# A Nystrom-attention and two-MLP kernel: heads grouped by parity, landmark products as eight 64x32 tiles, first q and k transposed a head at a time

## The chip, the cores and the metric

The kernel runs on one core of a Trainium2 chip. The metric is the device time of one execution in microseconds (us). Before the change the median of 3 runs is 896.05 us (895.35 to 901.98). About 1% (9 us) is what a measurement of this kernel can tell from no change.

## The reference

Nystrom attention with 32 landmarks per head feeds two MLPs; 4 batches, 8 heads of 64, 576 positions, all fp32.

```python
def _attn_ref(q, k, v):                      # (4, 8, 576, 64)
    q_lm = q.reshape(B, H, 32, 18, D).mean(axis=3)
    k_lm = k.reshape(B, H, 32, 18, D).mean(axis=3)
    A, Bm, C = sm(q, k_lm), sm(q_lm, k_lm), sm(q_lm, k)   # scaled softmax
    Z = Bm.T / (norm1(Bm) * norm_inf(Bm) + 1e-06)
    for _ in range(6):
        Z = 2 * Z - Z @ Bm @ Z
    return A @ Z @ C @ v
x = attn_out                                  # (2304, 512)
h = x @ w_in;   x = (h * sigmoid(h)) @ w_out              # 512 -> 2048 -> 512
h = x @ w2_in;  out = (h * tanh(softplus(h))) @ w2_out
```

## The kernel before, in words

**Stages.** A batch (b = 0 to 3) is two units (g = 0, 1) of four heads, and a unit is two pairs p of two heads. Per unit: q and k are loaded and transposed so that the head dimension lies on the partitions (tiles qT, kT); landmark sums (lm, qb); the product c of landmark queries with all keys; its softmax; a transposition of it (cp, ct); norms and the product with v (nb, cv); six Newton steps (nw, rv; attn_newton, L411); a last product wk, from which wt is made; and beside it the product a of all queries with landmark keys, transposed and normalised into ath (and its low part atl).

**Landmark products.** A is never multiplied with the 512 columns of the attention's output. u_steps (L518) multiplies wt, one row block of Z C v per head, into the first MLP's input weights: for every pair jp of 128-column blocks of w_in (8 pairs, 4 batches, so 32 blocks of work), a tile u of 128 x 512 in one PSUM bank. A tile wt holds two heads on 128 partitions, block-diagonal: wk is computed for both partition halves (L441), and the mask own2 (L446) keeps each head's own half, so half of what L531 multiplies is zero. Each u_steps call makes eight fp32 matmuls with 128 rows, 64 columns of weights and 128 moving columns; an fp32 matmul is two passes in the trace, so 16 rows of L531 a call. The result is copied by ACT (L541 for b = 0; for the others L546 as the rounded high part uw, and DVE's subtraction L548 as the low part).

**First MLP.** For b = 0, ha (L628) multiplies uf with ath, and ya (L829) multiplies the activated blocks gs with w_out, in two turns over 16 blocks; y_out writes the sums. For b = 1 to 3 the values are split in high and low parts (fp32r), and each block step t of the main loop has six passes h (L608), the activation on ACT, DVE and POOL, and twelve passes y (L608). Weights come as float64 words and are converted by POOL, ACT and DVE (L590 to L599) in three raw buffers; wsplit_stream (L790) splits w_out for b = 1 on (wh, wl). convert2 converts the second MLP's weights to DRAM in the background. The second MLP (hh, o) follows from about 480 us on and is not touched, but for a tile's name.

**What sets the order.** All of b = 0, b = 1 and the conversions is written as streams of steps with planned costs and dependencies, and interleave (L45) picks at each turn the step with the lowest score: when it could begin, plus WASTE times the idle time it would make, plus the stream's delay (the last number of each entry at L843 to L866). The program's order on every engine is what it picked; each engine then runs its own list in order. In the main loop u_all (L551) calls u_steps for the next batch in every second step, and attention steps of the batch after that run between (banks 5 and 7).

**Transpositions of b = 0.** attn_transposes (L219) makes, per half tile (96 x 3 rows of two heads), six fp32 matmuls against the identity, the two heads into partitions 0 to 63 and 64 to 127 of one bank (L242), and one ACT copy of 128 x 288 (L248). There are 16 half tiles, 8 a unit. From b = 1 on, both heads go in one PE transposition (L246). The q half tiles of a unit use one bank and the k half tiles another.

## Time and profile before

| | |
|---|---|
| median of 3 runs | 896.05 us |
| the profiled execution | 899.86 us, of which the span from its first to its last instruction is 898.1 us |
| busy share: PE, DVE, ACT, POOL | 96%, 73%, 53%, 33% |
| mean granted TensorE clock | 0.982 of full speed |

The profiled execution is 3.8 us above the median. An instruction row has its start, its duration, its engine, line and tiles. [...]

### The profile page before, as it was taken

How to read it: one execution, taken by the hardware profiler on the slowest of the kernel's cores; microseconds unless marked ns; L12 is line 12 of the kernel's file. 1: busy time of each engine (PE TensorE's matmuls, PEld its weight loads, DVE VectorE, ACT ScalarE, POOL GpSimd, SP SyncE). 2: the span in 40 equal slices, each digit the busy share in tenths (PEclk: the TensorE clock that was granted, in tenths of full speed). 3: DMA queues.
4: the chain of work that ended last, by engine and by line, in shares of the span. 5: the costliest groups of instructions: out<-in, count | busy, mean ns of one | idle time of the engine just before them, and what ended most of it. 6: DMA issues, size and time to landing. Idle time of an engine off the chain costs nothing.

```text
span 898.1 us, 15048 instructions
## 1 busy us (share of the span) xinstructions
PE 863.3 (96%) x5440; PEld 762.3 (85%) x5440; DVE 651.1 (73%) x1265; ACT 472.7 (53%) x1013; POOL 293.9 (33%) x334
## 2 busy tenths in 40 slices
PE   7799989999999998899999999999999999999997
PEld 5567767779998998899899889899999999999896
DVE  3878858676576968742364997787787787797776
ACT  3656546345344646653564555554554554555544
POOL 2211333015343545532433542242242242242221
PEclk8899989999999999999999999999999999999999
DMA  8645663433454576720562210110110110000000
GB/s 230 169 97 169 189 192 101 81 81 88 100 149 101 143 224 222 244 87 17 161 181 68 79 45 1 36 35 1 36 36 1 37 36 1 35 1 1 36 1 35
DMA packets 95354, 79.62 MB, mean 89 GB/s; under 512 B 52528, under 2 KB 80688, under 8 KB 95280
## 3 DMA queue, kind: packets, MB, share of 16 engines
q1 hardware_dynamic: 95280, 78.67, 30.6%
q8 instruction: 42, 0.69, 0.3%
q14 instruction: 32, 0.26, 0.1%
HBM read 60.82 MB, written 17.83 MB: 88 GB/s over the span
## 4 chain that ended last, share of the span: by engine, by line
PE 79%; DVE 8%; DMA 5%; ACT 3%; POOL 2%; issue 2%; SPq 1%; ACTq 0%; DVEq 0%; POOLq 0%
PE hh L608 21%; PE o L1098 20%; PE y L608 14%; PE h L608 7%; PE ya L829 5%; PE u L531 4%; PE ha L628 3%; DMA q<-in_q_dram 2%; PE nw L423 1%; DVE z L1036 1%; DMA w2r<-w2c 1%; DMA k<-in_k_dram 1%; PE cv L374 1%; POOL rawt L590 1%; PE c L307 1%
## 5 line engine op out<-in xcount | busy, mean ns | idle before, releaser
L1042 POOL TENSOR_TENSOR g<-z,g 128x384 fp32r<-128x384 f32 x94 | 96.0, 1022 | 256.0 <-ACT g L1039 253.6
L608 PE MATMUL y<-g,wh 128*128 128x288 f32 x768 | 162.4, 302 | 6.8 <-ACT g L659 2.9
L1098 PE MATMUL o<-wh,g 128*128 128x512 f32 x576 | 165.7, 395 | 2.9 <-ACT g L1039 1.9
L660 POOL TENSOR_TENSOR g<-g,g 128x288 fp32r<-128x288 f32 x96 | 82.4, 858 | 184.9 <-ACT g L659 143.0
L608 PEld LDWEIGHTS y<-g,wh 128*128 128x128 f32 x768 | 124.5, 190 | 12.0 <-ACT g L659 3.1
L608 PE MATMUL hh<-yl,wi2h 128*128 128x384 f32 x384 | 129.6, 337 | 0.0
L608 PE MATMUL hh<-yh,wi2h 128*128 128x384 f32 x384 | 129.2, 336 | 0.0
L608 PE MATMUL hh<-yh,wi2l 128*128 128x384 f32 x384 | 129.1, 336 | 0.0
L1098 PEld LDWEIGHTS o<-wh,g 128*128 128x128 f32 x576 | 106.0, 188 | 23.3 <-ACT g L1039 4.1
L1039 ACT CAST g<-z 128x384 fp32r<-128x384 f32 x96 | 49.3, 514 | 133.6 <-DVE z L1038 133.6
L608 PE MATMUL y<-g,wl 128*128 128x288 f32 x384 | 114.6, 298 | 0.0
L1025 DVE TENSOR_SCALAR e<-hh 128x384 f32<-128x384 f32 x96 | 53.5, 557 | 64.2 <-PE hh L608 63.9
L608 PE MATMUL h<-ath,uw 128*128 128x288 f32 x384 | 95.1, 302 | 0.0
L658 DVE SCALAR_TENSOR_TENSOR g<-th,h 128x288 f32<-128x288 f32 x96 | 43.0, 447 | 55.8 <-ACT th L657 54.3
L1098 PE MATMUL o<-wl,g 128*128 128x512 f32 x288 | 81.7, 391 | 0.0
L1026 ACT ACTIVATE e<-e 128x384 f32<-128x384 f32 x96 | 50.4, 525 | 51.4 <-DVE e L1025 51.2
L608 PEld LDWEIGHTS hh<-yl,wi2h 128*128 128x128 f32 x384 | 72.1, 188 | 3.7
L608 PEld LDWEIGHTS hh<-yh,wi2h 128*128 128x128 f32 x384 | 72.1, 188 | 3.7
L608 PEld LDWEIGHTS y<-g,wl 128*128 128x128 f32 x384 | 73.0, 190 | 0.0
L1036 DVE SCALAR_TENSOR_TENSOR z<-z,r 128x384 f32<-128x384 f32 x96 | 70.0, 729 | 3.3
L608 PEld LDWEIGHTS hh<-yh,wi2l 128*128 128x128 f32 x384 | 72.1, 188 | 0.0
L608 PEld LDWEIGHTS h<-ath,uw 128*128 128x128 f32 x384 | 68.1, 191 | 3.6 <-issue 3.0
(165 smaller groups left out, 1631.7 us busy)
## 6 DMA issues: line engine op xcount, KB each, us to landing
rawi<-in_moe_w_in_dram SPq DMA_DIRECT2D x16, 512.0 KB, 5.6
rawo<-in_moe_w_out_dram SPq DMA_DIRECT2D x16, 512.0 KB, 3.6
rawt<-in_moe_w_in_dram SPq DMA_DIRECT2D x16, 512.0 KB, 4.7
w2c<-ct SPq DMA_DIRECT2D x32, 256.0 KB, 2.6
rawt<-in_moe_w_out_dram SPq DMA_DIRECT2D x16, 512.0 KB, 3.8
w2r<-w2c SPq DMA_DIRECT2D x32, 256.0 KB, 2.8
v<-in_v_dram SPq DMA_DIRECT2D x32, 144.0 KB, 3.1
ysc<-yo SPq DMA_DIRECT2D x32, 144.0 KB, 1.9
```

Source lines behind the costliest of these rows:

```text
L531: pe.matmul(ub[64 * p : 64 * p + 64, jj, g], wt[:, p].rearrange("a h m -> a (h m)"), wc[2 * jp + jj][:, (2 * g + p) * P : (2 * g + p + 1) ...
L608: pe.matmul(o, a, b_, start=first and i == 0, stop=last and i == n - 1)
L628: pe.matmul(hb[:, :HB], uw[j // 2][:, j % 2, g], ath[0][:, g, hf * HB : (hf + 1) * HB], start=g == 0, stop=g == 1)
L658: dve.scalar_tensor_tensor(g2, th, 1.0, hb[:, :HB], op0=ALU.add, op1=ALU.mult)
L660: eng.tensor_tensor(gl, g2, gh.bitcast(F32), op=ALU.subtract)
L829: pe.matmul(yb[hf, m][:, :HB], wof[j][:, m * P : (m + 1) * P], gst[j // 2][:, j % 2, hf], start=j == 0, stop=j == NF - 1,)
L1025: dve.tensor_scalar(e, h, 20.0, None, op0=ALU.min)
L1026: ins = act.activation(e, e, AF.Exp)
L1036: dve.scalar_tensor_tensor(z, z, -2.0, r, op0=ALU.add, op1=ALU.mult)
L1039: act.copy(gh, z)
L1042: eng.tensor_tensor(gl, z, gh.bitcast(F32), op=ALU.subtract)
L1098: pe.matmul(obank[i][c], a[:, c * P : (c + 1) * P], w, start=j == 0 and k == 0, stop=j == NF - 1 and k == 2,)
```

## The change

Heads are put in units by parity: unit g has the heads 2i + g, so a 128-row block of w_in holds one head of each unit, that of unit 0 on partitions 0 to 63 and that of unit 1 on 64 to 127. wk is then computed for one half only and copied without a mask, and u_steps makes eight fp32 matmuls with 64 rows, 32 columns of weights and 256 moving columns: four heads give four column strips, two units two row halves and two PSUM banks, a bank each. The two blocks of w_in of a pair lie in one tile (wcp, first_in). Each call's two banks are copied by two ACT instructions of 128 x 256 in place of one of 128 x 512, and subtracted by two of DVE. The transpositions of b = 0 become PE transpositions of one head each (64 x 96, six a half tile), into partitions 0 to 63 of two banks; ACT copies one, DVE the other, each 64 x 288. Banks of the transpositions: (0, 6), (1, 7) for unit 0's q and k, (3, 5), (4, 5) for unit 1's. The planner's WASTE and most delays are other numbers, which moves work in the first 200 us.

```diff
-WASTE = 1.33
+WASTE = 0.7
...
-        h0 = 4 * g + 2 * p
+        heads = [2 * (2 * p + h2) + g for h2 in range(2)]
...
-                yield Step([("pe", 0.55 if b == 0 else 0.3)], deps)
+                if b == 0:
+                    yield Step([("pe", 0.5), ("dve", 0.4)], deps, ("tr", b, g, nm, p, hf))
+                else:
+                    yield Step([("pe", 0.3)], deps)
...
-                pt = bank(bk, f"tr{u}{p}{ti}{hf}")
-                for r in range(3):
-                    c = 3 * hf + r
-                    cols = slice(r * PT, (r + 1) * PT)
-                    if b == 0:
+                halves = slice(hf * HB, (hf + 1) * HB)
+                if b == 0:
+
+                    pts = [bank(bk[h2], f"tr{u}{p}{ti}{hf}{h2}") for h2 in range(2)]
+                    for r in range(3):
                         for h2 in range(2):
-                            pe.matmul(
-                                pt[64 * h2 : 64 * h2 + 64, cols], src[:, h2, c, :], ident[:PT, :PT], start=True, stop=True
+                            pe.transpose(
+                                pts[h2][:D, r * PT : (r + 1) * PT], src[:, h2, 3 * hf + r, :], ident[:PT, :PT]
                             )
-                    else:
-                        pe.transpose(pt[:, cols], src[:, c].rearrange("a h d -> a (h d)"), ident[:PT, :PT])
-                yield Step([("act", 0.4)], (), ("tr", b, g, nm, p, hf))
-                act.copy(dst[:, hf * HB : (hf + 1) * HB], pt[:, :HB])
+                    act.copy(dst[:D, halves], pts[0][:D, :HB])
+                    dve.tensor_copy(dst[D:, halves], pts[1][:D, :HB])
+                else:
+                    pt = bank(bk, f"tr{u}{p}{ti}{hf}")
+                    for r in range(3):
+                        pe.transpose(
+                            pt[:, r * PT : (r + 1) * PT],
+                            src[:, 3 * hf + r].rearrange("a h d -> a (h d)"),
+                            ident[:PT, :PT],
+                        )
+                    yield Step([("act", 0.4)], (), ("tr", b, g, nm, p, hf))
+                    act.copy(dst[:, halves], pt[:, :HB])
...
-        for i in range(n):
-            for h2 in range(2):
-                pe.matmul(wk[64 * h2 : 64 * h2 + 64, i, :P], rv[:, i, w:], bt["bb", i], start=True, stop=True)
+        for i, g in enumerate(gs):
+            pe.matmul(wk[64 * g : 64 * g + 64, i, :P], rv[:, i, w:], bt["bb", i], start=True, stop=True)
         yield Step([("dve", 0.3)], (), ("wt", b, gs[-1]))
         for i, g in enumerate(gs):
             pl, tag = (wp, f"gt{g + 1}") if b == 0 else (ap, f"wt{g}")
-            wt = pl.tile([P, 2, 2, M], F32, tag=tag, name=f"wt{b}{g}")
-            dve.tensor_tensor(
-                wt,
-                wk[:, i, :P].rearrange("a (p h m) -> a p h m", p=2, h=2),
-                own2[:, None, :, None].to_broadcast([P, 2, 2, M]),
-                op=ALU.mult,
-            )
+            wt = pl.tile([P, 4, M], F32, tag=tag, name=f"wt{b}{g}")
+            sl = slice(64 * g, 64 * g + 64)
+            dve.tensor_copy(wt[sl].rearrange("a h m -> a (h m)"), wk[sl, i, :P])
             units[b, g]["wt"] = wt
...
-            deps += [("wc", 2 * jp), ("wc", 2 * jp + 1), ("ath", 0, 1)] + ([("u", 0, jp - 2)] if jp > 1 else [])
+            deps += [("wc", 2 * jp), ("wc", 2 * jp + 1), ("ath", 0, 1)] + ([("u", 0, jp - 1)] if jp else [])
         elif b == 1:
             deps += [("y", 1, 2 * jp + 1)] + ([("u", 1, jp - 2)] if jp > 1 else [])
-        yield Step([("pe", 0.9)], deps)
-        ub = atbank(f"u{b}{jp}").rearrange("a (j g f) -> a j g f", j=2, g=2)
-        for g in range(2):
-            wt = units[b, g]["wt"]
-            for jj in range(2):
-                for p in range(2):
-                    pe.matmul(
-                        ub[64 * p : 64 * p + 64, jj, g],
-                        wt[:, p].rearrange("a h m -> a (h m)"),
-                        wc[2 * jp + jj][:, (2 * g + p) * P : (2 * g + p + 1) * P],
-                        start=True,
-                        stop=True,
-                    )
+        yield Step([("pe", 0.5)], deps)
+        ub = [atbank(f"u{b}{jp}{g}") for g in range(2)]
+
+        for h in range(4):
+            for g in range(2):
+                sl = slice(64 * g, 64 * g + 64)
+                pe.matmul(
+                    ub[g][32 * h : 32 * h + 32, : 2 * P].rearrange("a (j f) -> a j f", j=2),
+                    units[b, g]["wt"][sl, h],
+                    wcp[jp][sl, :, h * P : (h + 1) * P],
+                    start=True,
+                    stop=True,
+                )
         if b == 0:
-            yield Step([("act", 0.6)], (), ("u", 0, jp))
+            yield Step([("act", 0.8)], (), ("u", 0, jp))
             uw[jp] = wp.tile([P, 2, 2, P], F32, tag=f"u{jp}", name=f"uf{jp}")
-            act.copy(uw[jp], ub)
+            for g in range(2):
+                act.copy(uw[jp][:, g].rearrange("a j f -> a (j f)"), ub[g][:, : 2 * P])
             return
-        yield Step([("act", 0.6)])
+        yield Step([("act", 0.8)])
         ut = wp.tile([P, 2, 2, 2, P], F32R, tag=f"g{jp}", name=f"uw{b}_{jp}")
         uh, ul = ut[:, 0], ut[:, 1]
-        act.copy(uh, ub)
-        yield Step([("dve", 0.7)], (), ("u", b, jp))
-        dve.tensor_tensor(ul, ub, uh.bitcast(F32), op=ALU.subtract)
+        for g in range(2):
+            act.copy(uh[:, g].rearrange("a j f -> a (j f)"), ub[g][:, : 2 * P])
+        yield Step([("dve", 0.8)], (), ("u", b, jp))
+        for g in range(2):
+            dve.tensor_tensor(
+                ul[:, g].rearrange("a j f -> a (j f)"),
+                ub[g][:, : 2 * P],
+                uh[:, g].bitcast(F32).rearrange("a j f -> a (j f)"),
+                op=ALU.subtract,
+            )
         uw[jp] = (uh, ul)
...
+    wcp = {}
+
+    def first_in(j):
+
+        if j // 2 not in wcp:
+            wcp[j // 2] = wp.tile([P, 2, 512], F32, tag=f"wc{j // 2}", name=f"wc{j // 2}")
+        return wcp[j // 2][:, j % 2]
...
-            pe.matmul(hb[:, :HB], uw[j // 2][:, j % 2, g], ath[0][:, g, hf * HB : (hf + 1) * HB], start=g == 0, stop=g == 1)
+            pe.matmul(hb[:, :HB], uw[j // 2][:, g, j % 2], ath[0][:, g, hf * HB : (hf + 1) * HB], start=g == 0, stop=g == 1)
...
-            streams += [(attn_transposes(units[0, g], ti, 3 * g + ti), Banks(), (1.35, 0.06)[g])]
+            streams += [(attn_transposes(units[0, g], ti, ((0, 6), (1, 7), (3, 5), (4, 5))[2 * g + ti]), Banks(), (1.19, 0.25)[g])]
-    streams += [(u_steps(0, jp), Banks(6 + jp % 2), 0.38 + 0.05 * jp) for jp in range(NF // 2)]
+    streams += [(u_steps(0, jp), Banks(6, 7), 0.46 + 0.02 * jp) for jp in range(NF // 2)]
-    streams += [(u_steps(1, jp), Banks((3, 4)[jp % 2]), 1.24) for jp in range(NF // 2)]
+    streams += [(u_steps(1, jp), Banks(*((3, 7), (4, 5))[jp % 2]), 0.92) for jp in range(NF // 2)]
...
-                    hi = wp.tile([P, ND, P], F32R, tag=f"wc{j}", name=f"wi2h{j}")
+                    if j % 2 == 0:
+                        his = wp.tile([P, 2, ND, P], F32R, tag=f"wc{j // 2}", name=f"wi2h{j}")
+                    hi = his[:, j % 2]
```

Two places of the new order. The first is DVE in the six Newton steps of b = 0 (rv01 is unit 1's step value and rv00 unit 0's, nw the product that it is added to; mx, ath: softmax and result of the product a; rawi1: a weight conversion). Before:

```order
L435 TENSOR_TENSOR rv001_550<-nw001_549,rv000_539 128x64
L435 TENSOR_TENSOR rv011_555<-nw011_554,rv010_546 128x64
L435 TENSOR_TENSOR rv002_560<-nw002_559,rv001_550 128x64
L435 TENSOR_TENSOR rv012_565<-nw012_564,rv011_555 128x64
L435 TENSOR_TENSOR rv003_570<-nw003_569,rv002_560 128x64
```

And now:

```order
L444 TENSOR_TENSOR rv011_567<-nw011_566,rv010_556 128x64
L505 STREAM_TRANSPOSE ath0_580<-ta00_446 128x576
L444 TENSOR_TENSOR rv002_572<-nw002_571,rv001_563 128x64
L444 TENSOR_TENSOR rv012_577<-nw012_576,rv011_567 128x64
L496 TENSOR_REDUCE mx01_558<-ta01_532 128x18
L497 TENSOR_SCALAR mx01_558<-mx01_558 128x18
L498 RECIPROCAL mx01_558<-mx01_558 128x18
L444 TENSOR_TENSOR rv003_587<-nw003_586,rv002_572 128x64
L444 TENSOR_TENSOR rv013_590<-nw013_589,rv012_577 128x64
L607 SCALAR_TENSOR_TENSOR rawi1_182<-rawi1_182 128x512
L611 SCALAR_TENSOR_TENSOR wc0_260<-rawi1_182 128x512
L444 TENSOR_TENSOR rv014_600<-nw014_599,rv013_590 128x64
```

Softmax steps of the product a and a weight conversion, which stood ahead of the Newton steps or behind them, now stand between them.

The second is DVE at the end of b = 0, where the second turn of ya is over and the main loop begins (uw1_7 is the low part for pair 7 of b = 1, wl1 a split of w_out, yo1 the sums of ya, g20 the first activation of the main loop). Before, from pair 6 on, with attention steps of b = 2 (lm20, qb20) among them:

```order
L548 TENSOR_TENSOR uw1_6_1779<-u16_1765,uw1_6_1779 128x512
L682 TENSOR_SCALAR yo1_0_1795<-ya10_1190 128x288
L682 TENSOR_SCALAR yo1_2_1801<-ya12_1531 128x288
L797 TENSOR_TENSOR wl1_14_1781<-wl0_14_1433,wh1_15_1793 128x512
L293 TENSOR_TENSOR qb20_1961<-lm20_1705,mask2_86 128x128
L300 TENSOR_SCALAR lk20_1964<-lm20_1705 128x64
L595 SCALAR_TENSOR_TENSOR rawt0_2355<-rawt0_2355 128x512
L548 TENSOR_TENSOR uw1_7_1808<-u17_1784,uw1_7_1808 128x512
```

And now, from pair 5 to g20 (each pair has two rows, a bank each); ahead of them, behind the last yo1, stand the rows of the pairs 3 and 4 and one more split:

```order
L555 TENSOR_TENSOR uw1_5_1820<-u150_1808,uw1_5_1820 128x256
L555 TENSOR_TENSOR uw1_5_1820<-u151_1809,uw1_5_1820 128x256
L814 TENSOR_TENSOR wl1_12_1818<-wl0_12_1402,wh1_13_1837 128x512
L555 TENSOR_TENSOR uw1_6_1839<-u160_1827,uw1_6_1839 128x256
L555 TENSOR_TENSOR uw1_6_1839<-u161_1828,uw1_6_1839 128x256
L607 SCALAR_TENSOR_TENSOR rawt0_2411<-rawt0_2411 128x512
L555 TENSOR_TENSOR uw1_7_1853<-u170_1842,uw1_7_1853 128x256
L555 TENSOR_TENSOR uw1_7_1853<-u171_1843,uw1_7_1853 128x256
L814 TENSOR_TENSOR wl1_14_1862<-wl0_14_1445,wh1_14_1860 128x512
L814 TENSOR_TENSOR wl1_14_1862<-wl0_14_1445,wh1_15_1864 128x512
L611 SCALAR_TENSOR_TENSOR ct0_2643<-rawt0_2411 128x512
L676 SCALAR_TENSOR_TENSOR g20_1877<-th0_1876,h0_1868 128x288
```

What moved: the subtractions of five pairs, four splits of w_out and a conversion now stand between the last ya and the main loop, and the attention steps of b = 2 behind them.

## Rows read from the trace of the kernel before

**Rows 1.** PE over the whole span: busy time (share of the span) and instructions, from the page.

```profile
PE 863.3 (96%) x5440; PEld 762.3 (85%) x5440; DVE 651.1 (73%) x1265; ACT 472.7 (53%) x1013; POOL 293.9 (33%) x334
```

**Rows 2.** Stretches: length, busy of PE, PEld, DVE, ACT, POOL, granted clock, DMA.

```profile
60.00:80.00 20.00, 18.41 (x115) 12.53 (x113) 16.21 (x34) 11.79 (x27) 2.91 (x5) 1.00 0.58 142
...
270.00:300.00 30.00, 30.00 (x264) 26.42 (x263) 19.94 (x44) 15.39 (x38) 11.66 (x14) 1.00 0.46 123
380.00:425.00 45.00, 45.00 (x396) 42.33 (x395) 18.00 (x32) 20.41 (x46) 14.06 (x18) 1.00 0.18 62
```

**Rows 3.** Two DMA waits in the chain that ended last: start, length, what.

```profile
115.87 3.35 DMA rawo<-in_moe_w_out_dram
...
123.72 4.75 DMA k<-in_k_dram
```

**Rows 4.** PE timeline around two landmark blocks, one in b = 0, one for b = 2.

```profile
80.00 1.09 PE L531 MATMUL u<-wc,wt 128*64 128x128 f32 x16
81.02 4.15 PE L628 MATMUL ha<-ath,uf 128*128 128x288 f32 x16
85.00 0.49 PE L358 MATMUL cp<-ident,ce 128*96 128x128 f32 x3
...
297.95 1.09 PE L531 MATMUL u<-wc,wt 128*64 128x128 f32 x16
298.98 0.53 PE L608 MATMUL y<-g,wh 128*128 128x288 f32 x2
```

**Rows 5.** Groups by line on DVE: the subtraction of u, the nearest rows (busy us, mean ns).

```profile
L1031 DVE TENSOR_TENSOR e<-n,hh 128x384 f32<-128x384 f32 x96 | 53.2, 554 | 3.3
...
L548 DVE TENSOR_TENSOR uw<-u,uw 128x512 fp32r<-128x512 f32 x24 | 16.5, 688 | 13.0 <-ACT uw L546 13.0
...
L797 DVE TENSOR_TENSOR wl<-wl,wh 128x512 fp32r<-128x512 f32 x16 | 10.9, 682 | 0.7 <-ACT wh L794 0.6
```

**Rows 6.** Timeline of PE and its weight loads in transpositions of b = 0 (L242) and b = 1 (L246).

```profile
22.63 1.14 PEld L242 LDWEIGHTS tr<-ident,q 96*64 96x64 f32 x12
...
23.59 1.14 PEld L242 LDWEIGHTS tr<-ident,k 96*64 96x64 f32 x12
...
133.97 0.69 PE L246 MATMUL tr<-ident,q 96*128 96x96 f32 x3
134.45 0.58 PE L246 MATMUL tr<-ident,k 96*128 96x96 f32 x3
```

**Rows 7.** Stretches: the granted clock (behind the engines) while those transpositions ran.

```profile
22.00:24.00 2.00, 2.00 (x29) 2.00 (x28) 1.18 (x2) 1.25 (x5) 0.00 (x0) 0.50 0.88 281
...
128.00:134.00 6.00, 5.39 (x14) 3.88 (x15) 1.00 (x2) 0.40 (x1) 1.93 (x3) 0.50 0.61 229
```

**Rows 8.** Timeline of the Newton steps of b = 0: first pair of products, ACT copies, first landmark block.

```profile
42.34 6.78 PE L423 MATMUL nw<-rv 128*128 128x192 f32 x20 [2.96 <-DVE rv L435]
...
44.00 0.27 ACT L434 COPY rv<-nw 128x128 f32<-128x128 f32 x1 [0.64 <-PE nw L423]
...
45.62 0.27 ACT L434 COPY rv<-nw 128x128 f32<-128x128 f32 x1 [0.64 <-PE nw L423]
...
46.88 0.27 ACT L434 COPY rv<-nw 128x128 f32<-128x128 f32 x1 [0.35 <-PE nw L423]
...
48.11 0.27 ACT L434 COPY rv<-nw 128x128 f32<-128x128 f32 x1 [0.35 <-PE nw L423]
...
50.50 1.09 PE L531 MATMUL u<-wc,wt 128*64 128x128 f32 x16
```

**Rows 9.** PE timeline from the last ya to the first y of the main loop.

```profile
190.33 1.72 PE L829 MATMUL ya<-gs,wl 128*128 128x288 f32 x6
191.98 1.09 PE L531 MATMUL u<-wc,wt 128*64 128x128 f32 x16
...
194.00 1.19 PE L465 MATMUL a<-qT,qb 128*64 128x288 f32 x8
...
198.24 0.69 PE L608 MATMUL y<-g,wh 128*128 128x288 f32 x2
```

More of the change, by code (lines that the diff above doesn't have):

```diff
@@ L123, in nystrom_moe_kernel @@
     sel2 = cp.tile([P, 2], F32, name="sel2")
-    own2 = cp.tile([P, 2], F32, name="own2")
     blk = cp.tile([P, P], F32, name="blk")
     two = cp.tile([P, 1], F32, name="two")
-    for t in (mask2, mask4, sel2, own2, blk):
+    for t in (mask2, mask4, sel2, blk):
         pool.memset(t, 0.0)
@@ L193, in load_part @@
                             t[o : o + 32, hf * n : hf * n + n],
-                            src[b, h0 + h2, hf * HB : (hf + 1) * HB, M * dh : M * dh + M].rearrange(
+                            src[b, heads[h2], hf * HB : (hf + 1) * HB, M * dh : M * dh + M].rearrange(
                                 "(c p) d -> p c d", p=M
@@ L203, in load_part @@
                 sp.dma_start(
-                    t[:, h2] if apart else t[:, :, h2, :], src[b, h0 + h2].rearrange("(p c) d -> p c d", c=NC)
+                    t[:, h2] if apart else t[:, :, h2, :], src[b, heads[h2]].rearrange("(p c) d -> p c d", c=NC)
                 )
@@ L633, in h1_matmuls @@
         for g in range(2):
-            wh, wl = uh[:, j % 2, g], ul[:, j % 2, g]
+            wh, wl = uh[:, g, j % 2], ul[:, g, j % 2]
             xh, xl = ath[b][:, g, sl], atl[b][:, g, sl]
@@ L772, in out @@
         def out():
-            wc[j] = wp.tile([P, 512], F32, tag=f"wc{j}", name=f"wc{j}")
-            return wc[j]
+            return first_in(j)
         yield from raw_steps(raws.pop(("i", j)), out, (), ("ci", j))
@@ L847, in nystrom_moe_kernel @@
     order = [(1, g, nm, p) for g in range(2) for nm, p in (("q", 0), ("k", 0), ("q", 1), ("k", 1), ("v", 0), ("v", 1))]
-    streams += [(head_load(*it), Banks(), 1.31) for it in order]
-    streams += [(first_unit(0, 0), Banks(0, 1, 2), 0.38), (first_unit(0, 1), Banks(3, 4, 5), 0.05)]
+    streams += [(head_load(*it), Banks(), 1.4) for it in order]
+    streams += [(first_unit(0, 0), Banks(0, 1, 2), 0.43), (first_unit(0, 1), Banks(3, 4, 5), 0.07)]
     for g in range(2):
-        streams += [(queries(units[0, g]), q01, (0.32, 0.25)[g])]
+        streams += [(queries(units[0, g]), q01, (0.66, 0.52)[g])]
@@ L852, in nystrom_moe_kernel @@
         for ti in range(2):
-            streams += [(attn_transposes(units[0, g], ti, 3 * g + ti), Banks(), (1.35, 0.06)[g])]
-    streams += [(u_steps(0, jp), Banks(6 + jp % 2), 0.38 + 0.05 * jp) for jp in range(NF // 2)]
-    streams += [(h_stream(j, hf), Banks(), 0.59 + 0.01 * (2 * j + hf)) for j in range(NF) for hf in range(2)]
+            streams += [(attn_transposes(units[0, g], ti, ((0, 6), (1, 7), (3, 5), (4, 5))[2 * g + ti]), Banks(), (1.19, 0.25)[g])]
+    streams += [(u_steps(0, jp), Banks(6, 7), 0.46 + 0.02 * jp) for jp in range(NF // 2)]
@@ L856, in nystrom_moe_kernel @@
+    streams += [(h_stream(j, hf), Banks(), 0.85 + 0.01 * (2 * j + hf)) for j in range(NF) for hf in range(2)]
     streams += [(win_stream(j), Banks(), 1.08 + 0 * j) for j in range(NF)]
-    streams += [(y_stream(), Banks(), 1.18)]
-    streams += [(wout_stream(j), Banks(), 1.17 + 0.05 * j) for j in range(NF)]
+    streams += [(y_stream(), Banks(), 1.19)]
+    streams += [(wout_stream(j), Banks(), 1.28 + 0.02 * j) for j in range(NF)]
     for g in range(2):
-        streams += [(attn_transposes(units[1, g], ti, 4 + ti), Banks(), (0.75, 0.87)[g]) for ti in range(2)]
-        streams += [(second_attention(g), a1, (0.67, 1.15)[g])]
-        streams += [(attn_softmax(units[1, g]), a1, (1.36, 0.66)[g])]
@@ L863, in nystrom_moe_kernel @@
-    streams += [(u_steps(1, jp), Banks((3, 4)[jp % 2]), 1.24) for jp in range(NF // 2)]
-    streams += [(wsplit_stream(j), Banks(), 2.0) for j in range(NF)]
+        streams += [(attn_transposes(units[1, g], ti, 4 + ti), Banks(), (0.74, 1.05)[g]) for ti in range(2)]
+        streams += [(second_attention(g), a1, (1.14, 0.98)[g])]
+        streams += [(attn_softmax(units[1, g]), a1, (1.24, 1.67)[g])]
+    streams += [(u_steps(1, jp), Banks(*((3, 7), (4, 5))[jp % 2]), 0.92) for jp in range(NF // 2)]
@@ L865, in nystrom_moe_kernel @@
+    streams += [(wsplit_stream(j), Banks(), 1.48) for j in range(NF)]
     attn2 = attn_batch(2)
```

2 lines of the change are left out of this document (removed).

## The prediction

> **What bounds the kernel now.** I read the page's busy shares first: PE has 863.3 of 898.1 us, 96% [rows 1], so a second taken from PE counts wherever PE has no wait to fill it, and the other engines matter where they make PE wait. The table of stretches says where that is [rows 2]. In 270 to 300 us (landmark blocks for b = 2 among the steps of b = 1) and in 380 to 425 us (those for b = 3) PE is busy in all of the 30.00 and 45.00 us at full clock, DVE in 19.94 and 18.00 of them: time taken from PE there is time off the end. In 60 to 80 us (blocks of b = 0) PE has 18.41 of 20, DVE 16.21: nearly so. The chain of waits shows that the first 130 us hold waits of another kind, for transfers: 3.35 us for w_out at 115.87 and 4.75 us for a k at 123.72 [rows 3]. What PE saves ahead of these can be lost in them.
>
> **The landmark blocks on PE.** Before, a block is 16 passes of 128 columns and takes 1.02 us from its start to the start of what follows (80.00 to 81.02; 297.95 to 298.98 with 1.03) [rows 4]. What one pass costs alone is in the same group: 16 passes of 288 columns with the whole array take 85.00 - 81.02 = 3.98 us, 0.249 each, 0.86 ns a column, so 128 columns are 0.111 us and 16 passes one by one 1.77. The block took 1.02: the two column halves run side by side, 8 x 0.111 = 0.89, and 0.13 for start and drain.
>
> After the change a block is 16 passes of 256 columns, 0.221 each, on eight tiles: four column strips, two row halves. The trace shows two column halves side by side, never four strips, and never two row halves. So the ends are: all eight side by side, 2 x 0.221 + 0.13 = 0.57 (0.45 saved); strips side by side but row halves in turn, 4 x 0.221 + 0.13 = 1.01 (nothing saved); two at a time as now, 8 x 0.221 + 0.13 = 1.90 (0.88 lost). I take 0.62, a saving of 0.40: the halves that the rows show overlap entirely, which is nearest to all eight; 0.05 is for the loads of eight tiles in place of two before the first passes. For 32 blocks the ends are -14.4 and +28.2 us, and the value -12.8, if all of it counts.
>
> It does not count everywhere. For b = 2 and b = 3, 16 x 0.40 = **-6.4**; PE there had no idle time [rows 2], and the blocks still stand one to every second step. Each takes both background banks now (5 and 7), so an attention step behind it has to wait for its eviction; the steps of b = 3's attention come some us later, and b = 3's own blocks have none behind them. I cost that at nothing; without this cover it is under 1.5 us for each of the few blocks that have one close behind.
>
> For b = 0, 8 x 0.40 = 3.2, of which I count **-2.5**, since PE is busy 18.41 of 20 us there [rows 2] and the waits of [rows 3] lie ahead; the ends are -3.2 and 0.
>
> **Evictions.** Two instructions of 256 columns replace one of 512. On DVE the subtraction takes 0.688 us at 512 columns, and a subtraction-like row from PSUM at 384 columns 0.554 [rows 5], 1.05 ns a column, so 256 columns are 0.42 and the two 0.84: +0.15 a block on DVE, 3.6 us over 24 blocks, and about as much on ACT (53% busy [rows 1]). In the main loop that is hidden behind PE: DVE has 7 of 30 us free or more [rows 2]. It isn't hidden at the end of b = 0's stage:
>
> **The end of b = 0.** The second order piece puts five pairs' subtractions, four splits of w_out, two conversion steps and two sums yo1 between the last ya and the main loop's first g20. In DVE time: 5 x 0.84 + 4 x 0.68 + 2 x 0.69 (nearest row of that shape) + 2 x 0.45 = 9.2 us, then g20 itself and its split in front of the first y: near 11 us from the last ya to the first y. PE has only five blocks (5 x 0.6) and three h groups (0.8 each) for that time, 5.4 us, and waits for the rest. Before, this stretch was 191.4 (the end of six ya passes from 190.33) to 198.24, 6.8 us, and held one block, three h groups and the products a (194.00) and c of b = 2, about 2.4 us together [rows 9]. So the stretch is 4 us longer, and 2.4 us of PE work is put off into the main loop, where PE is full: +6.4. In return four blocks less stand ahead of it (4 x 1.02 = 4.1) and three are 0.40 shorter (1.2): -5.3. Net **+1**; the eight blocks' own 3.2 us are lost here. The ends: -3 if DVE is as far ahead at the last ya as before, +4 if ACT's casts come late as well.
>
> **The start.** A half tile was 12 passes of 96 columns in 23.59 - 22.63 = 0.96 us, at a granted clock of 0.50 [rows 6, 7]: two heads side by side, 0.16 each. It is now six PE transpositions, all into partitions 0 to 63. Three such transpositions of 96 columns take 134.45 - 133.97 = 0.48 us at the same clock [rows 6, 7], 0.16 each: six are 0.96. PE gains nothing. The copy is shared by ACT and DVE, and the q and k half tiles of unit 1 share bank 5, so each has to wait for DVE's copy of the one before: some 0.3 us on seven half tiles, +2. Then the Newton steps: the first order piece puts softmax steps of a and a conversion of rawi1 (two steps of about 0.7 us) between the sums. Two neighbouring steps (one of each unit) took 45.62 - 44.00 = 1.62 us at half clock and 48.11 - 46.88 = 1.23 at full [rows 8]; in 1.23 us DVE has some 0.45 to do, so some 4 us of added DVE work lengthen the chain by 1 to 2. In return, what now stands inside it stood ahead of unit 1's first product at 42.34 [rows 8], which I expect 1 to 2 us earlier relative to its inputs. Together **+1**, from -2 to +5.
>
> [...] In the trace PE was busy in all of 22 to 24 us at a clock of 0.50 [rows 7], and the Newton pairs went from 1.62 to 1.23 us when it rose [rows 8]. [...]
>
> The smaller wk and the copy of wt without a mask I cost at nothing: a pass or two a batch, behind DVE.
>
> **Sum.** -6.4 - 2.5 + 1 + 1 = -6.9. The profiled execution took 899.86 us, so it would be 893.0; the median of the runs is 3.8 below that execution, 896.05, and gives 889.2. I forecast 889.2 as a median, 886 to 893 by itself.
>
> **The rivals.** First, all counts: the start gains what its banks cost, DVE is ahead at the end of b = 0, and the order packs the transfer waits. -12.8, and a quarter of the two waits of [rows 3] (2 us): near 881. For it: the sum of the blocks is that large. Against: the second order piece.
>
> Second, four strips but not two rows: blocks take 1.01 and the change does not do what it says. The main loop and b = 0 gain nothing; the end of b = 0 is +6.4 - 4.1 = +2.3 (the five longer blocks lie in PE's wait), the start +1: 899.4. For it: no row shows row halves side by side.
>
> Third, the clock: the stage from the transpositions to the landmark products runs at 0.50. The Newton steps' six pairs cost 0.39 us more each, of which half did already, and the products ahead of them as much again: +4, so 893. [...]
>
> Fourth, slower: only two of the eight tiles ever run at once. A block is 1.90 us, +0.88 in 24 to 32 blocks, +21 to +28: near 922. It decides from the point where fewer than four passes run side by side. Against it: the pairs of column halves overlap without loss [rows 4].
>
> **How the numbers follow.** 1% (9 us) is what a measurement can tell, so faster is below 887.1 and slower above 905.0. Chances: the forecast 0.45, all counts 0.23, two rows in turn 0.12, the clock 0.14, slower 0.06. Of the forecast some 0.10 lies below 887.1. Faster 0.33, the same 0.61, slower 0.06. The range leaves out the fourth rival, the far side of the first and some of the second: 880 to 900.
>
> **What would show it.** Blocks of 0.6 us between their start and the next group's; 1.0 or 1.9 decides for the second or fourth rival. PE full in the main loop, and the stretch with b = 3's blocks 3.2 us shorter. A PE gap of 4 to 6 us behind the last ya, ended by DVE. The first landmark block near 51 to 52 us, where it was at 50.50 [rows 8]; a granted clock of 0.50 up to there is the third rival. I am wrong if blocks take 0.6 and the total doesn't fall, or if the first 200 us change by more than 5 us either way.

## The result, and the profile after

The changed kernel takes 908.73 us (median of 7 runs, 905.23 to 910.35), the kernel before 896.41 beside it (7 runs, 895.35 to 901.98). The ratio is 1.0112, with a 95% interval from 1.0083 to 1.014: slower by 1.1%, 19.5 us above the forecast of 889.2 and outside its range. The profiled execution is the longest of the seven and has a span of 908.6 us.

PE over the whole span after the change, from the page, answers [rows 1]:

```profile
PE 864.0 (95%) x5328; PEld 746.0 (82%) x5328; DVE 658.4 (72%) x1305; ACT 475.4 (52%) x1045; POOL 293.8 (32%) x331
```

PE is as busy as before in a span 10.5 us longer. The stretches that answer [rows 2] (the last one is that with the blocks of b = 3, which now begin at 386.79 and not at 382.0):

```profile
60.00:80.00 20.00, 20.00 (x134) 14.46 (x127) 17.00 (x30) 13.90 (x36) 2.65 (x4) 0.86 0.59 150
270.00:300.00 30.00, 30.00 (x247) 27.36 (x244) 18.36 (x51) 10.47 (x30) 6.69 (x9) 0.94 0.35 81
395.00:435.00 40.00, 35.56 (x306) 30.50 (x306) 27.27 (x47) 24.86 (x60) 18.59 (x22) 0.96 0.57 196
```

The prediction had PE full in the main loop. It is not: 35.56 of 40.00 us in the last row (one wait of 3.88 us at 412.66, for DVE's sums yo, is most of the gap), and a clock under 1.00 in all three. Yet the blocks themselves came out as forecast. PE timeline around two of them, answering [rows 4]:

```profile
80.80 0.66 PE L535 MATMUL u<-wc,wt 64*32 64x256 f32 x16
81.39 2.94 PE L646 MATMUL ha<-ath,uf 128*128 128x288 f32 x11
...
286.24 0.72 PE L535 MATMUL u<-wc,wt 64*32 64x256 f32 x16
286.89 0.40 PE L620 MATMUL y<-g,wh 128*128 128x288 f32 x1
```

From a block's start to the next group's it is 0.59 and 0.65 us, where 0.62 was forecast and 1.02 stood before (a row reaches past the next start: 80.80 + 0.66 is 81.46, and ha starts at 81.39). That is near the prediction's estimate for all eight tiles side by side (0.57) and far from that for row halves in turn (1.01). So the time went elsewhere. The table cuts the span at four starts on PE's timeline, with three experiments of the next section beside it. Each column is one profiled execution, and its sum need not be that of the median.

| stretch (us) | before | after | loads first | loads first, own2 back | before, loads behind |
|---|---|---|---|---|---|
| start to the first y | 198.2 | 196.9 | 193.4 | 193.8 | 191.0 |
| first y to the first block of b = 2 | 77.2 | 89.3 | 79.1 | 79.1 | 90.6 |
| from there to the first hh | 209.9 | 206.6 | 204.4 | 203.2 | 203.4 |
| first hh to the last group of o | 408.3 | 411.2 | 411.1 | 408.5 | 408.3 |

Two rows lose: the first 77 us of the main loop (+12.1) and the last stage (+2.9). The first stretch differs by several us between executions: up to the first landmark block "after" and "loads first" have the same order and are 2.3 us apart, and in the kernel before and two of the next section that differ from it only behind this stretch or by one small tile the first y comes at 198.2, 192.8 and 195.3. So its terms can't be told apart to a microsecond.

The start answers [rows 6, 8]. One of the seven half tiles that wait for DVE's copy of the one before, and the end of the Newton steps:

```profile
21.06 1.01 PE L243 MATMUL tr<-ident,k 96*64 96x96 f32 x5 [0.38 <-DVE qT__283 L247]
...
57.58 1.02 PE L449 MATMUL wk<-bb,rv 128*64 128x128 f32 x4
58.97 1.11 PE L535 MATMUL u<-wc,wt 64*32 64x256 f32 x16 [0.38 <-DVE wt L455]
```

Six of the seven waits are 0.38 or 0.39 us, where some 0.3 was forecast, and one is 0.76: 3.1 us together. The first landmark block is 8.5 us later than before; 5.5 of that stand ahead of the run of Newton products (47.88, where it was 42.34), 2.9 inside it.

The first loss is in SP's queue. SP's transfers (start, length, what), the kernel before ahead of the changed one:

```profile
155.71 1.91 SPq L684 DMA_DIRECT2D ysc<-yo  x4
157.66 3.97 SPq L192 DMA_DIRECT2D q<-in_q_dram  x8
```

```profile
153.63 4.07 SPq L702 DMA_DIRECT2D ysc<-yo  x4
166.07 1.74 SPq L201 DMA_DIRECT2D v<-in_v_dram  x4
186.65 3.00 SPq L702 DMA_DIRECT2D ysc<-yo  x4
189.70 3.98 SPq L190 DMA_DIRECT2D q<-in_q_dram  x8
```

The q at 157.66 and at 189.70 is the same load, the first of batch 2's attention. Before, it stands behind the four stores of yo0 only. After, it stands behind the four of yo1 as well, and these wait for the last ya, whose last pass starts at 186.3. No data holds the load back (with the loads first it is issued at 154.08, below); it is the place in the queue. The planner's entry delay of this stream (8.0) is the same in both kernels, and the order around it moved past it. The load is 32 us later than before, batch 2's attention follows it, and the main loop, which has to have that finished before the first block of b = 2, lets PE wait for its chain of small steps. PE's timeline there after the change:

```profile
263.68 0.29 PE L620 MATMUL h<-ath,uw 128*128 128x288 f32 x1
264.64 0.43 PE L383 MATMUL cv<-v,ct 96*64 96x128 f32 x2 [0.67 <-ACT ct L369]
266.10 0.43 PE L374 MATMUL nb<-bc,blk 128*128 128x64 f32 x2 [1.03 <-DVE bc L354]
266.46 0.44 PE L383 MATMUL cv<-v,ct 96*64 96x128 f32 x4
267.74 0.64 PE L378 MATMUL nb<-bc,bb 128*128 128x32 f32 x2 [0.84 <-DVE bb L356]
268.31 2.40 PE L383 MATMUL cv<-v,ct 96*64 96x128 f32 x18
```

and the stretch around it (PE has 15.40 of 18.00, at a mean clock of 0.81):

```profile
256.00:274.00 18.00, 15.40 (x103) 12.76 (x100) 14.34 (x34) 7.89 (x20) 7.31 (x9) 0.81 0.24 46
```

The reader is to see two prices: waits of 0.67, 1.03 and 0.84 us on small instructions of ACT and DVE, and behind them a clock at 0.50, at which the 18 products of cv take 2.33 us until h follows at 270.64. From the first y to the first block of b = 2 PE is busy 85.47 of 89.30 us at a mean clock of 0.95 (before, 77.11 of 77.12 at 1.00). An estimate of the 12.1 us from these: 3.8 of waits, some 4.2 of low clock (0.50 for 8.4 us, the first 1.6 of them at the start of the main loop), 2.4 for products a and c that now stand here, and the rest mostly a few more passes of h and y.

### The profile page after: what moved, and what is told of

Its sections match the earlier page's. It is cut to its first block, busy times and chain, and to the rows that moved or that the text cites. A ratio compares the mean times of both kernels' runs of the same rounds, so it can differ in the third digit from the quotient of the medians.

```text
span 908.6 us, 14945 instructions
## 1 busy us (share of the span) xinstructions
PE 864.0 (95%) x5328; PEld 746.0 (82%) x5328; DVE 658.4 (72%) x1305; ACT 475.4 (52%) x1045; POOL 293.8 (32%) x331
## 4 chain that ended last, share of the span: by engine, by line
PE 70%; DVE 10%; issue 6%; ACT 4%; DMA 4%; POOL 4%; SPq 0%; POOLq 0%; ACTq 0%; DVEq 0%
PE hh L620 20%; PE o L1117 20%; PE y L620 10%; PE h L620 5%; PE ha L646 3%; PE ya L846 3%; POOL g L678 2%; DMA rawo<-in_moe_w_out_dram 2%; PE u L535 2%; DMA rawt<-in_moe_w_in_dram 1%; PE tr L243 1%; DVE z L1055 1%; PE nw L432 1%; POOL rawt L602 1%; PE a L469 1%
## 5 line engine op out<-in xcount | busy, mean ns | idle before, releaser
L620 PE MATMUL y<-g,wh 128*128 128x288 f32 x768 | 164.3, 303 | 7.1 <-DVE yo L700 3.9
L1045 ACT ACTIVATE e<-e 128x384 f32<-128x384 f32 x96 | 50.3, 524 | 54.8 <-DVE e L1044 54.4
L675 ACT ACTIVATE th<-h 128x288 f32<-128x288 f32 x96 | 39.2, 409 | 69.1 <-PE h L620 69.0
```

What stands on the lines that cost most here:

```text
L620: pe.matmul(o, a, b_, start=first and i == 0, stop=last and i == n - 1)
L675: tanhs.append(act.activation(th, hb[:, :HB], AF.Tanh, scale=0.5))
L1045: ins = act.activation(e, e, AF.Exp)
```

## The experiments

**Loads first.** One number of the changed kernel.

```diff
-    streams += [(attn2, Banks(5, 7), 8.0, True)]
+    streams += [(attn2, Banks(5, 7), 4.0, True)]
```

> The changed kernel with one number changed: the stream of batch 2's attention enters with a delay of 4.0 in place of 8.0, so that its first q and k loads stand ahead of the four stores of yo1 in SP's queue, and not behind them. Theory (SP's queue: the loads wait behind stores that wait for the last ya): the loads are issued near 150 to 160 us and not at 189.70, from the first y to the first landmark block of b = 2 the time falls from 89.3 back to 77 to 80 us, the PE gap at 263.7 to 270.6 goes, and the total falls by 8 to 12, to 897 to 901. Rival (the attention of b = 1 is late by 10 us and DVE is full): the earlier loads change the total by less than 3.

Measured: 893.66 us (892.06 to 896.49), ratio to before 0.9968 (0.995 to 0.9986). 15 us less than the changed kernel, where 8 to 12 was expected. SP's queue, PE at the products that it waited for, and the stretch:

```profile
151.12 2.91 SPq L702 DMA_DIRECT2D ysc<-yo  x4
154.08 3.98 SPq L190 DMA_DIRECT2D q<-in_q_dram  x8
```

```profile
255.51 0.36 PE L378 MATMUL nb<-bc,bb 128*128 128x32 f32 x2
256.09 1.60 PE L383 MATMUL cv<-v,ct 96*64 96x128 f32 x24 [0.22 <-ACT ct L369]
```

```profile
256.00:274.00 18.00, 17.91 (x159) 16.74 (x160) 14.47 (x40) 7.94 (x21) 5.76 (x8) 1.00 0.60 138
```

The load is issued at 154.08, the waits shrink to 0.22, the clock stays at 1.00, and the stretch to the first block is 79.1 us. The theory of SP's queue holds, the rival (b = 1's attention is late anyway) falls. Not all of it need be the queue's: of the 16.0 us between the two profiled executions 10.2 lie in this stretch and 2.2 in the one behind it, but 3.5 lie ahead of the first y, 2.3 of them already at the first landmark block.

**Before, loads behind.** The same number turned the other way in the kernel before.

```diff
-    streams += [(attn2, Banks(5, 7), 8.0, True)]
+    streams += [(attn2, Banks(5, 7), 20.0, True)]
```

> The kernel before with the one number turned the other way: the stream of batch 2's attention enters with a delay of 20.0 in place of 8.0, so that its first q and k loads stand behind the four stores of yo1 in SP's queue, as they do in the changed kernel. Theory (SP's queue alone makes the main loop late): the loads are issued near 190 us and not at 157.66, from the first y to the first landmark block of b = 2 it takes 86 to 90 us and not 77.2, and the total rises by 8 to 15, to 906 to 913. Rival (it costs only together with the change's late attention of b = 1): the total rises by less than 4.

Measured: 904.05 us (898.94 to 907.25), ratio 1.0066 (1.0039 to 1.0092). The load is issued at 187.60 and the stretch to the first block takes 90.6 us (+13.4), a little over the expected 86 to 90. The total rises by 5.9 by the medians, between the theory (8 to 15) and the rival (under 4). The profiled execution, 899.69, is one of the shortest of the ten, with the first y at 191.0, so it shows where the loss goes and not the median's size. In it the stretch behind is 6.5 us shorter. In 340 to 380 us, where the kernel before let PE wait, the deferred work leaves fewer gaps (first row: before; second: loads behind):

```profile
340.00:380.00 40.00, 33.45 (x251) 31.72 (x251) 32.59 (x66) 24.52 (x56) 23.97 (x26) 0.96 0.73 238
```

```profile
340.00:380.00 40.00, 36.54 (x279) 32.66 (x278) 32.40 (x73) 23.96 (x56) 21.20 (x23) 1.00 0.57 185
```

So the late load alone makes a kernel slower, without anything else of the change; some half of the loss can come back later. In the changed kernel it did not come back: there the stretch behind is 2.2 us longer than with the loads first.

**Transpositions as matmuls.** The new transpositions in the same order, but not in PE's transposition mode.

```diff
-                            pe.transpose(
-                                pts[h2][:D, r * PT : (r + 1) * PT], src[:, h2, 3 * hf + r, :], ident[:PT, :PT]
+                            pe.matmul(
+                                pts[h2][:D, r * PT : (r + 1) * PT], src[:, h2, 3 * hf + r, :], ident[:PT, :PT], start=True, stop=True
```

> The changed kernel with the transpositions of the first q and k issued as plain matmuls against the identity, into the same places of the same banks, in the same order. Theory (transpositions in PE's own mode leave the clock low, the third rival of the prediction): the granted clock rises near 29 us and not at 38, the first landmark block comes at 54 to 57 us and not at 58.97, and the total falls by 1 to 3. Rival (PE waits for the copies, and the clock follows the waits): the clock's rise and the first block stay within 1 us, the total within 1.

Measured: 909.41 us (908.84 to 913.37), 0.7 from the changed kernel. The first landmark block starts at 58.75, where it was 58.97. The clock in the Newton steps, first the changed kernel, then this one:

```profile
48.00:58.00 10.00, 8.63 (x25) 5.57 (x26) 6.84 (x19) 2.86 (x10) 2.31 (x2) 0.52 0.07 17
```

```profile
48.00:58.00 10.00, 8.67 (x25) 5.58 (x24) 6.33 (x18) 2.86 (x10) 2.28 (x2) 0.50 0.09 27
```

The low clock in the Newton steps is there either way, behind a wait of PE for DVE's rv of 3.25 us in the changed kernel (up to 47.88) and of 3.30 here. Earlier the two kernels do differ. From 26 to 30 us, while unit 1's q and k are transposed, the run with the loads first (PE's own mode, same order up to there) and this one, with PE busy as long in both:

```profile
26.00:30.00 4.00, 2.93 (x16) 1.88 (x14) 1.17 (x3) 1.22 (x4) 1.22 (x2) 0.50 0.85 179
```

```profile
26.00:30.00 4.00, 2.90 (x32) 2.52 (x32) 2.15 (x4) 0.78 (x2) 1.30 (x2) 1.00 1.11 332
```

The changed kernel's own trace holds no clock record before 38.1 us, but by its pace it ran at the low level too: four passes of c take 0.98 us at 34.34 there, and 0.50 at 34.27 here. So the clock did change, as the theory had it, and the time did not: the first block is 0.2 us earlier and not 2 to 5, since a half tile is six passes in PE's own mode (0.96 us from 6.18 in the changed kernel, 0.16 each, as in the three of b = 1 at 0.50 [rows 6, 7]) and twelve as matmuls (0.99 from 10.03 here, at 1.00), and the waits for the copies stay. The two levels of 26 to 30 us (0.50 against 1.00) are those of one execution each; what makes PE's own mode run at the lower one was not shown. Plain matmuls do not make the high clock sure: before the change they ran at 0.50 from 22 to 24 us [rows 7].

**Old transpositions, new order.** Loads first, and two heads transposed into one bank by matmuls and copied by ACT, as before.

```diff
-                    pts = [bank(bk[h2], f"tr{u}{p}{ti}{hf}{h2}") for h2 in range(2)]
...
-                    act.copy(dst[:D, halves], pts[0][:D, :HB])
-                    dve.tensor_copy(dst[D:, halves], pts[1][:D, :HB])
+                    pt = bank(bk[0], f"tr{u}{p}{ti}{hf}")
...
+                    act.copy(dst[:, halves], pt[:, :HB])
```

> The changed kernel with batch 2's loads ahead of the stores of yo1 (as in the run with the loads first) and with the first q and k transposed as before: two heads into one bank, copied by ACT. Against the run with the loads first only the transpositions differ. Theory (the start's 8.5 us are mostly taken back by the transfers that bound the first 130 us, as the end of ha, later by only 2.4, says): the first landmark block at 51 to 53 us, the total 1 to 3 below the run with the loads first. Rival (the start counts in full): 6 to 9 below it.

Measured: 896.75 us, but spread from 891.61 to 903.33; 3.1 above the run with the loads first, and neither theory has it above; what makes it so is open, and the profiled execution, 891.61, is the shortest of the ten. The first block is at 55.3 us, and not at 51 to 53; with the new transpositions and the same delays it comes between 55.9 and 59.0 in five profiles. So the transpositions by themselves do not make most of the start late. But the comparison is not clean: from the same delays the planner makes another order here (unit 0's Newton products start at 30.10, before unit 1's nb and cv).

**Blocks alone.** Old transpositions and all old delays; only the landmark products and the heads by parity are new.

```diff
-WASTE = 0.7
+WASTE = 1.33
...
-    streams += [(u_steps(0, jp), Banks(6, 7), 0.46 + 0.02 * jp) for jp in range(NF // 2)]
+    streams += [(u_steps(0, jp), Banks(6, 7), 0.38 + 0.05 * jp) for jp in range(NF // 2)]
...
```

> The landmark products as eight tiles and the heads by parity, as in the changed kernel, but the first q and k transposed as before (two heads into one bank, copied by ACT) and every delay of the order and WASTE as before. The prediction's own terms without start and end: -6.4 for b = 2 and 3 and -2.5 for b = 0 give 886 to 890. Rival (the saving needs the new order, since DVE's or ACT's evictions or the transfers set the end in the first 200 us and the main loop has waits that grow): 893 to 898. Both expect blocks of 0.6 us and the first landmark block near 50.5 to 51.5.

Measured: 898.11 us (895.54 to 901.61), ratio 1.0007 (0.999 to 1.0024): no gain, as the rival had it (893 to 898; the prediction's terms gave 886 to 890), and the first block at 50.34. By the trace the main loop (first y to first hh) takes 284.6 us where before took 287.1, and the last stage loses 3.0 (own2 is gone here too; see the last two runs). In the main loop one wait stands out:

```profile
303.71 0.66 PE L535 MATMUL u<-wc,wt 64*32 64x256 f32 x16
...
310.05 0.89 PE L367 MATMUL cp<-ident,ce 128*96 128x128 f32 x3 [3.90 <-DVE uw L555]
```

A block holds both background banks, and the next attention step waits 3.90 us until they are evicted; the prediction had under 1.5 for such a case.

**Transpositions, old order.** The new transpositions and blocks with all old delays (the numbers of the diff above and the rest of the table).

> The changed kernel with every delay of the order and WASTE as before; the new transpositions and the new landmark products stay. With the run of the blocks alone (old transpositions, old order) and the two with the loads first it makes a square of two by two. Theory (the late start comes from the new order, not from the transpositions: with the old transpositions in the new order the first landmark block came at 55.3 us, in the old order at 50.3): the first block at 51 to 53 us, the end of ha within 3 us of 105.2, the total 897 to 900. Rival (each half tile of unit 1 waits for DVE's copy, 1.55 us in place of 0.96): the first block at 54 us or later and the total above 900.

Measured: 915.91 us (914.96 to 916.45), ratio 1.0178 (1.0146 to 1.0211), the first block at 69.99. The rival's figures hold: without the new order the new transpositions cost 17.8 us against the blocks alone. Its reason is only a part: PE's waits for DVE's copies are 3.8 us up to the first block, which is 19.7 later. The granted clock is 0.50 in all of 40 to 75 us, where the blocks alone have 1.00 from 46 on, and the planner makes another order of the same delays: unit 1's Newton products begin at 60.46, behind unit 0's last, where the blocks alone run both side by side from 41.91. How the loss divides stays open. In the new order the first block comes at 56.7 (new transpositions) or 55.3 (old). The new delays repair what the new transpositions break, and cost the old ones some 5 us at the first block.

**Before, two banks.** The block of the kernel before, evicted from two banks in the main loop.

```diff
+        if b > 1:
+            pair = [atbank(f"u{b}{jp}{x}") for x in range(2)]
...
+            for g in range(2):
+                act.copy(uh[:, :, g], pair[g][:, : 2 * P].rearrange("a (j f) -> a j f", j=2))
...
```

> The kernel before, with one thing of the change alone: a landmark block of the main loop (b = 2 and 3) writes its two halves into both background banks, 5 and 7, and is evicted by two instructions on ACT and two on DVE; its 16 passes stay 128 columns wide. Theory (a block that holds both banks makes the next attention step wait for its eviction: PE waited 3.9 us for the block's subtraction with the blocks alone): PE waits of 2 to 5 us for that subtraction between 300 and 325 us, and the total 2 to 5 above before. Rival (PE's queue has enough else to do, as the prediction had it): no such wait over 1 us, the total within 1 of before. Beside it: the last stage keeps the memory layout of before, and its 384-column passes should start 175.0 ns apart, as in the profile of before, and not 176.4 as in all kernels with the change.

Measured: 898.95 us (894.41 to 902.3), ratio 0.9999 (0.9975 to 1.0023), and no wait of PE for the subtraction. Holding two banks alone costs nothing, as the prediction had it; the theory falls. The last stage's passes are 175.0 ns apart, as before.

**No conversions between the blocks** (with the loads first) and **casts on DVE** (with the loads first and own2 back).

```diff
-        while cvn[0] < min(34, (18 * (t - 11) // 52 if t < 64 else t - 45)):
+        while cvn[0] < min(34, (18 * (min(t, 26) - 11) // 52 + 13 * max(0, t - 41) // 22 if t < 64 else t - 45)):
```

```diff
-            act.copy(uh[:, g].rearrange("a j f -> a (j f)"), ub[g][:, : 2 * P])
+            (dve.tensor_copy if b > 1 else act.copy)(uh[:, g].rearrange("a j f -> a (j f)"), ub[g][:, : 2 * P])
```

> The changed kernel with the loads first, and the second layer's conversions held between the 27th and the 42nd step of the main loop, where the blocks of b = 2 stand; they are made up after it. Theory (ACT reaches a block's casts late, since it waits in order for POOL's part of a conversion ahead of them): PE's wait of 1.85 us for the block's subtraction at 304.49 shrinks to under 0.5 and the total falls by 1 to 4, to 890 to 893. Rival (the conversions only move, and crowd DVE and the transfers at 340 to 376 us): the total stays or rises, 893 to 898.

> The changed kernel with the loads first and own2 put back, and the casts of the main loop's landmark blocks on DVE in place of ACT. Theory (ACT reaches the casts late behind the conversions, and the two background banks are held that long): the PE wait for the block's subtraction, 1.9 us near 304, goes under 0.5, total 1 to 3 below 890.3. Rival (DVE is as far behind there as ACT, or worse for the two more instructions a block): the wait stays at 1.5 or more, total 890 to 893.

Measured: 894.51 us (892.51 to 896.39) and 888.44 (887.84 to 889.86; ratio to before 0.9894, 0.9862 to 0.9925). The wait stays in both, 2.1 and 2.0 us. The first of the two does not test its theory: the trace still has five conversions end on DVE from 272 to 318 us (tile ct), as many as with the loads first, and two of them start at 300.49 and 302.88, beside the block at 300.62. PE's waits from 296 to 312 us with the casts on DVE (us in total, times, longest), and DVE's timeline (its line numbers are one higher than the changed kernel's):

```profile
PE cp L368 <- DVE uw L556: 2.0, 1, 2.0
```

```profile
301.55 1.77 DVE L612 SCALAR_TENSOR_TENSOR ct<-rawt 128x512 uint32<-128x512 uint32 x1
303.24 0.74 DVE L298 TENSOR_REDUCE lm<-qT 128x32 f32<-128x576 f32 x1
303.90 0.44 DVE L677 SCALAR_TENSOR_TENSOR g<-th,h 128x288 f32<-128x288 f32 x1
304.26 0.74 DVE L553 CAST uw<-u 128x256 fp32r<-128x256 f32 x2
304.93 0.74 DVE L556 TENSOR_TENSOR uw<-u,uw 128x256 fp32r<-128x256 f32 x2
```

The block ran at 300.73, and DVE comes to it at 304.26, behind a conversion of 1.77. So ACT is not the cause by itself: with the casts on DVE, its own queue stands in front of them. How the wait could be avoided stays open. Against before beside each, the casts on DVE (0.9894) are level with own2 put back alone (0.9895, next), so the 1.9 us between their medians is not shown to be a gain.

**own2 put back.** Loads first, and own2, a tile of 128 x 2, back: cleared, and read by nothing.

```diff
+    own2 = cp.tile([P, 2], F32, name="own2")
     blk = cp.tile([P, P], F32, name="blk")
```

> [...] Theory (the operands' addresses set the pace of the last stage): the 384-column passes start 175.0 ns apart again, and not 176.4, the last stage takes 408.3 us and not 411.1, and the total falls by 2 to 3, to 891. Rival (the pace is that of another execution, or of the paired tiles): 176.4 as before, total within 1 of 893.7.

Measured: 890.34 us (889.35 to 891.31), ratio to before 0.9895 (0.9863 to 0.9927); 3.3 less than without the tile. The last stage on PE, 540 to 840 us (length, PE busy and its passes, then the other engines, the clock): before, after, own2 back.

```profile
540.00:840.00 300.00, 300.00 (x1513) 271.99 (x1512) 239.81 (x433) 161.74 (x319) 90.41 (x88) 1.00 0.08 22
```

```profile
540.00:840.00 300.00, 300.00 (x1501) 271.18 (x1500) 238.72 (x431) 159.32 (x315) 90.27 (x88) 1.00 0.07 20
```

```profile
540.00:840.00 300.00, 300.00 (x1513) 271.76 (x1512) 239.47 (x432) 161.37 (x320) 90.19 (x88) 1.00 0.08 22
```

PE is busy all the time at full clock in all three, and does 0.8% fewer passes in the changed kernel (1499 with the loads first alone); with the tile it is back at 1513, the starts of two 384-column passes 175.0 ns apart and not 176.4. The theory's figures hold. That addresses are the cause is the author's reading: no trace here shows one.

**Before, shifted.** The reverse: one more such tile in the kernel before.

```diff
+    pad2 = cp.tile([P, 2], F32, name="pad2")
     blk = cp.tile([P, P], F32, name="blk")
```

> [...] Theory (addresses set the last stage's pace): its 384-column passes start 176.4 ns apart and not 175.0, the stage takes about 411 us and not 408.3, the total rises by 2 to 4. Rival (the changed kernel's other tiles matter too): 175.0, and the total within 1 of before.

Measured: 898.58 us (897.89 to 902.94), ratio 1.002 (1.0 to 1.0039).

```profile
540.00:840.00 300.00, 300.00 (x1508) 272.28 (x1507) 238.87 (x431) 161.45 (x319) 90.20 (x88) 1.00 0.08 22
```

Between the two: hh slows to 176.0 ns, the passes of o stay at 230.2 (232.3 in the changed kernel), and the stage takes 409.3 us, where about 411 was expected; the total does not move clear of noise. One such tile more or less changes the pace (1508 passes here, 1513 without it), but not by the same amount in both kernels; what decides is open.

## Why the prediction was wrong

Its sum was -6.9 us. With the two things that it did not contain put right (loads first, own2 back) the changed kernel takes 890.34, 8.3 below before beside it. So the terms held in sum, in part by luck (the start and the evictions were off, see below), and what failed is what had no term.

- *The blocks on PE: right.* 0.59 to 0.65 us where 0.62 was forecast. From the first block of b = 2 to the first hh the kernel with both put right takes 203.2 us, 6.7 less than before, where -6.4 was forecast. That it is so close is luck: PE's waits in that stretch changed too, and the blocks alone take 2.5 less there, with 3.90 in one wait.
- *"2.4 us of PE work is put off into the main loop": this step failed.* The order piece showed a and c of b = 2 leaving the end of b = 0. I read that as 2.4 us of PE's work that moves, on PE and DVE alone, and did not ask why they moved. They moved because their loads had gone behind four stores in SP's queue, and with them the whole chain of small steps behind the loads. The 2.4 us of work are there; the waits (3.8 us) and the low clock (some 4.2) had no term. The step cost 12.1 us in the first 77 of the main loop; taking the loads forward lowered the total by 15 us.
- *"PE full in the main loop": wrong.* It was read from two stretches that are full before and stay full with the loads first and own2 back (45.00 of 45.00 us in 377 to 422). In the changed kernel DVE's and ACT's free time hid nothing once PE's own queue held a chain of small dependent steps. And the kernel before was not full everywhere: 33.45 of 40.00 us in 340 to 380, a stretch that the prediction's rows leave out.
- *The evictions behind both banks, costed at nothing: mis-sized.* One wait of 1.35 to 3.90 us in the experiments with the new blocks (in the changed kernel, whose attention is late, three of 0.20 to 0.95), where "under 1.5" was the bound. It is not the banks alone (two banks in the kernel before cost nothing); the cause stays open.
- *The start, +1: wrong in its place, near in its sum.* The waits for DVE's copy are there, 3.1 us on seven half tiles where +2 was forecast. But the first block came at 58.97 and not at 51 to 52. The new delays are some 5 of it (55.3 against 50.3 with the old transpositions, though the order that follows differs in more than the delays). Of the 8.5 us, 6 were back by the end of ha (last pass at 104.3 against 101.9); 1.6 of these are a wait that is gone, since PE has 20.00 of 20.00 us in 60 to 80, where it had 18.41 [rows 2], and the rest is not worked out.
- *The end of b = 0: right, but for the gap.* From the start of the last ya pass (186.3) to the first y (196.9) it is 10.7 us, where near 11 was forecast. The prediction read the end of ya before as 191.4; by the start of that last pass (191.6) it was 6.6 us, so the stretch is 4.1 longer, where 4 was forecast. DVE ends the waits, but they are 0.54, 1.40 and 1.10 us, 3.0 together and not 4 to 6.
- *The third rival: right on the clock in part, wrong on its price.* With PE's own transpositions the clock is 0.50 at 26 to 30 us (loads first) and with plain matmuls 1.00, and from 38.1 to 48.4 us the changed kernel has 1.00; but the first block comes within 0.2 us and the total within 0.7. The clock of 0.50 in the Newton steps is there with plain matmuls too.
- *No term for a tile that goes.* Taking own2 away cost 2.6 us by the trace of the last stage, which the change does not touch, and 3.3 by the medians.

The change does what it says and is worth about 1%: the fastest version run, with the loads first, own2 back and the casts of b = 2 and 3 on DVE, takes 888.44 us, 0.9894 of before (own2 back without those casts: 0.9895).

## What to carry to other kernels

Where an order moves, read every queue, the DMA issuer's first: a load that needs nothing but is queued behind a store waits for whatever that store waits for, and the price is paid a stage later (here the load was issued at 189.70 us and not at 154.08, and the stretch up to the first block of b = 2 took 89.3 us and not 79.1). When a trace shows work that has merely "moved later", ask what released it before and what does now; the answer names the cost. A stage that the change leaves alone can still change its pace (here with one small tile gone: 1501 passes in 300 us, and 1513 before), so compare passes per microsecond there.

## What the runs showed of the hardware

One tile of 128 x 2 that nothing reads changed the pace of PE by 0.9%, at a clock of 1.00 and with PE busy in 300.00 of 300.00 us: 1499 passes from 540 to 840 us with the loads first, and 1513 with own2 back. The kernel before has 1513 there, and 1508 with one more such tile; one execution each.

Sixteen fp32 passes of 256 columns on eight tiles of 64 x 32 take 0.59 to 0.65 us in the changed kernel, from a block's start to the next group's. While PE transposed in its own mode the granted clock was 0.50 (loads first), with plain matmuls in the same places 1.00 (26 to 30 us, one execution each); a half tile took 0.96 us as six passes of its own mode in the changed kernel, at 0.50 by their pace, and 0.99 as twelve matmuls at 1.00.
